# Sliding-window attention and a gated MLP on one core: f16 transposes for q and k, loads a stage earlier, and a new order at the end of batch 0

## The chip, the cores and the metric

The kernel runs on one NeuronCore of a Trainium2 chip. The metric is the device time of one execution in microseconds. Eleven executions of the kernel before are given, with their median; beside them one execution was taken with the hardware profiler.

## What is computed

Eight batches of 576 tokens and eight heads of 64. Attention looks back over 64 tokens; its output is the input of a gated MLP whose gate mixes tokens with a 576 x 576 matrix.

```python
scores = (1/sqrt(64)) * q @ k.T               # per batch and head, 576 x 576
mask = (rel >= 0) & (rel < 64)                # rel = query position - key position
attn = softmax(where(mask, scores, -1e9))
x = (attn @ v)                                # heads side by side: 576 x 512
h = relu(x @ w_in)                            # 576 x 1024
u, w = h[:, :512], h[:, 512:]
w_n = (w - mean(w)) / sqrt(var(w) + 1e-6)     # per token
out = (u * (w_spatial @ w_n + b_spatial)) @ w_out
```

## The kernel before

**Units of work.** All matmuls are f16 with fp32 sums. For each batch the program has these units, named by the letters of its order strings:

- T (`emit_T`, L287): q and k of two heads are brought to the layout with the 64 head elements on partitions. T0 to T3 take a pair of heads' first 512 tokens, T4 the last 64 tokens of all. In batches 0 to 3 (`NPE` is 4, L60) this is done on TensorE. `load_four` (L82) lets each partition hold four neighbouring tokens, so slot t of partition p is token 4p + t. `T_mm` (L258) multiplies each slot's 128 x 128 block with the identity and writes fp32 to PSUM with a step of four, which restores the order of tokens; k and q have a PSUM tile each. `T_out` (L277) copies k with VectorE and q with ScalarE into the f16 tile `tr`. In batches 4 to 7 the DMA brings another layout and VectorE turns 32 x 32 blocks (`turn`, L144; its units are T in stage 3 and R later).
- A (`att`, L582): scores S, exp on ScalarE and mask on VectorE of one head pair, and with it P (`emit_P`, L388), the product with v, of the pair before, then its normalisation: Ln (`emit_N1`, L411) and exp (`N_exp`) on ScalarE, a product on VectorE (`N_mul`, L426), which writes `x`. P has one PSUM buffer `oz`, S one buffer `sc`. What of the normalisation is left is done by the next unit, or by F.
- V (`emit_V`, L472; in parts as p for `V_mm`, L451, and o for `V_out`, L462): the half of w_in that is normalised, relu on ScalarE and `bn_stats` on VectorE. Q (`emit_VO4`, L481) is the last 64 tokens of V, run beside those of the batch before's O. L (`emit_LN`, L503): normalisation, five `vn` on VectorE.
- U (L520): the ungated half. W (`emit_W`, L571): transposes of w_spatial, once, in batch 0. G (L539): the product with w_spatial and the gate. O (L561): the product with w_out, a ScalarE copy to `ob` (five buffers), a store from SyncE.

All PSUM tiles of T, V, U, G, O and W come from one ring `mm` of four banks.

**Order.** Nothing is planned by a scheduler: every engine runs its instructions in program order (`manual_schedule`, L40), and waits only for semaphores. A first loop (L671) runs the attention of batch 0, with some idle matmuls `warm` in between. After it L706 to L721 interleave the rest of batch 0 with the attention of batch 1. Then stage a (L723) runs the MLP of batch a with the attention of batch a + 1, by a string of units for each a (`run`, L600).

**Loads.** q, k and v of a batch are loaded by DMAs from SyncE's queue (`load_pairs`, L96, for the first four; `load_batch`, L133, for the others: 16 DMAs of q and k, five of v). GpSimd casts them to f16 and makes a copy of v that is shifted by 64 partitions (`batch_in`, L654). The fp32 buffers and those of v are double; the f16 buffers of q and k (`nk`, `nq`) are single, so a cast waits until T of the batch before has read its own. Batches 0 and 1 are loaded at once, 2 before L704; for batch a + 2 the unit Q of stage a issues load and casts (L627). The weights come by GpSimd's DMAs (`load_win`, L238; `load_wsp`, L242). SyncE's queue also carries the stores.

Of the kernel before, what the change touches and what calls it, by code (L numbers as in the profile page):

```python
# [13 lines left out]
B = 8  # L14
# [5 lines left out]
def kernel(  # L20
# [11 lines left out]
    nc = tc.nc  # L32
    f16 = dt.float16
    f32 = dt.float32
# [12 lines left out]
    psp = ctx.enter_context(tc.tile_pool(name="ps", bufs=1, space=bass.MemoryType.PSUM))  # L47
# [59 lines left out]
    def pairs_in(b, s, copy_k, copy_q):  # L107
        cast_four(b, "k", s, copy_k)
        cast_four(b, "q", s, copy_q)
# [128 lines left out]
    def load_win(half):  # L238
        cs = slice(512 * half, 512 * half + 512)
        nc.gpsimd.dma_start(w_in_sb[:, :, cs], moe_w_in[:, cs].rearrange("(r p) c -> p r c", p=128))  # L240
# [15 lines left out]
    TP = {}  # L256

    def T_mm(b, s):  # L258
        if s < 4:
            tp = [psp.tile([128, 512], f32, tag="mm", bufs=4, name=f"tp{b}_{s}{x}") for x in "kq"]  # L260
        else:
            tp = psp.tile([128, 512], f16, tag="mm", bufs=4, name=f"tp{b}_{s}")
        TP[b, s] = tp
        with nc.named_scope(f"T{b}_{s}"):
            for y, x in enumerate("kq"):
                w = NH[b, x, s]
                if s < 4:
                    o = tp[y][:, :].rearrange("p (n t) -> p t n", t=4)
                    for t in range(4):
                        nc.tensor.matmul(o[:, t, :], w[:, 128 * t:128 * t + 128], id16[:, :],  # L270
                                         start=True, stop=True)
                else:
                    for p in range(4):
                        nc.tensor.transpose(tp[:, 256 * y + 64 * p:256 * y + 64 * p + 64],
                                            w[0:64, 128 * p:128 * p + 128], id16[0:64, 0:64])

    def T_out(b, s):  # L277
        tp = TP.pop((b, s))
        o = TR[b][:, :, :].rearrange("p x (a n) -> p x a n", a=4)
        for y in (0, 1):  # L280
            if s < 4:
                (act_copy if y == 1 else dve_copy)(o[:, y, s, 0:512], tp[y][:, :])
            else:
                nc.vector.tensor_copy(o[:, y, :, 512:576],
                                      tp[:, 256 * y:256 * y + 256].rearrange("p (a n) -> p a n", a=4))
# [102 lines left out]
    def emit_P(b, s):  # L388
        oz = psp.tile([128, 2, 512], f32, tag="oz", bufs=1, name=f"oz{b}_{s}")
        OZ[b, s] = oz  # L390
        e2 = E2.pop((b, s))
        Vn, Vs = V16[b]
        n = 512 if s < 4 else 256
        with nc.named_scope(f"P{b}_{s}"):
            for h in (0, 1):
                nc.tensor.matmul(oz[64 * h:64 * h + 64, 1, 0:n], onesK[:, :], e2[:, h, 0:n],  # L396
                                 start=True, stop=True)
            for u in range(8 if s < 4 else 4):
                c0 = 64 * u if s < 4 else slot(b, u)
                for h in (0, 1):  # L400
                    if s < 4:
                        hh = 2 * s + h
                        vt = Vn[:, u // 2, hh, :] if u % 2 == 1 or u == 0 else Vs[:, u // 2, hh, :]
                    else:
                        vt = Vs[:, 4, 2 * u + h, :]
                    nc.tensor.matmul(oz[64 * h:64 * h + 64, 0, c0:c0 + 64],  # L406
                                     vt, e2[:, h, c0:c0 + 64], start=True, stop=True)
# [163 lines left out]
    def emit_W(kk):  # L571
        sn = 128 if kk < 4 else 64
        wps = psp.tile([128, 1024], f16, tag="mm", bufs=4, name=f"wps{kk}")
        for tch in range(5):
            tn = 128 if tch < 4 else 64
            nc.tensor.transpose(wps[0:sn, 128 * tch:128 * tch + tn],
                                wsp_nat[0:tn, tch, 128 * kk:128 * kk + sn], id16[0:tn, 0:tn])
        (act_copy if kk % 2 else dve_copy)(wspT[kk][0:sn, 0:576], wps[0:sn, 0:576])

    state = {"P": None, "post": []}  # L580

# [18 lines left out]
    def run(a, seq):  # L600
        for t in seq.split():
            c, n = t[0], int(t[1:] or 0)
            if c == "A":
                if a + 1 < B:
                    att(a + 1, n)
            elif c == "T":
                if a + 1 < NPE:
                    emit_T(a + 1, n)
                elif a + 1 < B:
                    for x in "kq":  # L610
                        turn(a + 1, x, n)
            elif c == "R":
                if a + 2 < B:
                    for x in "kq":
                        turn(a + 2, x, n)
            elif c == "F":
                for f in state["post"]:
                    f()
                state["post"] = []
            elif c == "p":  # L620
                V_mm(a + n // 1000, n // 100 % 10, n // 10 % 10, n % 10)
            elif c == "o":
                V_out(a, n)
            else:
                if c == "Q":
                    emit_VO4(a)
                    if a > 0 and a + 2 < B:  # L627
                        load_any(a + 2)
                        batch_in(a + 2)
                elif c == "L":  # L630
                    emit_LN(a)
                elif c == "W":
                    emit_W(n)
                else:
                    UNIT[c](a, n)
                if state["post"]:
                    state["post"].pop(0)()

    def load_any(b):
        if b < NPE:  # L640
            load_pairs(b)
        else:
            new_qkv(b)
            load_batch(b)

    def v_in(b, s):
        if s < 4:
            cast_v_pair(b, s, pool_copy)
            shift_pair(b, s, pool_copy)
        else:  # L650
            cast_v_chunk(b, 4, pool_copy)
            shift_rem(b, pool_copy)

    def batch_in(b):  # L654
        if b < NPE:
            for s in range(4):
                pairs_in(b, s, pool_copy, pool_copy)
                if s == 3:
                    pairs_in(b, 4, pool_copy, pool_copy)
                v_in(b, s)  # L660
            v_in(b, 4)
            return
        for hp in (0, 1):
            for x in "kq":
                cast_qk(b, x, hp, pool_copy)
        for c in range(5):
            cast_v_chunk(b, c, pool_copy)
            if c in (1, 3, 4):
                shift_part(b, c // 2, pool_copy)

    for s in range(4):  # L671
        pairs_in(0, s, dve_copy, pool_copy if s < 3 else dve_copy)
        if s == 3:
            pairs_in(0, 4, pool_copy, pool_copy)
        v_in(0, s)
        if s == 2:
            load_win(1)
            load_win(0)
        T_mm(0, s)
        if s < 3:  # L680
            warm(2)
        if s > 0:
            E_mask(0, s - 1)
        if s > 1:
            N_mul(0, s - 2)
        T_out(0, s)
        emit_S(0, s)
        E_exp(0, s)
        if s == 3:
            T_mm(0, 4)  # L690
        if s > 0:
            emit_P(0, s - 1)
            emit_N1(0, s - 1)
            N_exp(0, s - 1)
        if s < 3:
            warm(4)
# [6 lines left out]
    load_pairs(2)  # L703
    batch_in(1)  # L704

    run(0, "p0002 p0102")  # L706
    emit_P(0, 3)
    emit_S(0, 4)
    E_exp(0, 4)
    emit_N1(0, 3)  # L710
    emit_N2(0, 3)
    E_mask(0, 4)
    run(0, "p0202 p0302")
    emit_P(0, 4)
    run(0, "p0023 p0123 p0223 p0323 p0034 o0 p0134 o1 p0234 o2 p0334 o3")
    emit_N1(0, 4)
    emit_N2(0, 4)
    run(0, "U0 U1 Q L U2 T0 U3 A0 W0 W1 W2 W3 W4 U4 G0 T1 A1 G1 G2 T2 G3 A2 G4")
    batch_in(2)
    run(0, "O0 O1 T3 A3 O2 O3 T4 F A4 F p1002 p1102")  # L720
    run(0, "A5 p1202 p1302 p1023 p1123 p1223 p1323 F")  # L721
# [1 line left out]
    for a in range(1, B):  # L723
        if a == 1:
            run(a, "p0034 o0 p0134 o1 p0234 o2 p0334 o3 T0 U0 T1 U1 A0 Q L T2 U2 U3 A1 U4 G0 T3 A2 "
                   "G1 G2 T4 A3 G3 A4 G4 O0 O1 A5 O2 O3")
        elif a == 2:
            run(a, "V0 T0 V1 T1 A0 V2 V3 Q T2 A1 F L U0 U1 U2 T3 A2 U3 U4 G0 T4 A3 G1 G2 G3 A4 "
                   "G4 O0 O1 A5 O2 O3")
        elif a == 3:  # L730
            run(a, "V0 T0 V1 V2 V3 A0 Q F L T1 U0 U1 A1 U2 U3 U4 A2 G0 G1 A3 G2 G3 A4 G4 R0 O0 O1 "
                   "A5 O2 R1 O3")
        else:
            run(a, "V0 V1 A0 V2 V3 Q A1 F L U0 U1 U2 A2 U3 U4 G0 A3 G1 G2 G3 A4 G4 R0 O0 O1 A5 O2 R1 O3")
# [31 lines left out]
```

The softmax here doesn't subtract the row's maximum and nothing guards it: scores larger than these inputs give would overflow.

## Time and profile before

| | |
|---|---|
| median of 11 runs | 242.35 us (240.89 to 246.01) |
| the profiled execution | 245.4 us |
| its span, first to last instruction | 243.7 us |
| granted TensorE clock, mean | 0.958 |
| busy: TensorE, VectorE, ScalarE, GpSimd | 215.1, 153.9, 157.8, 114.4 us |
| DMA: q1 (SyncE's queue), of 16 engines' span | 69.9% |
| stages 1 to 6, from one Q to the next | 25.45, 24.48, 24.72, 23.58, 28.95, 22.42 us |

PE is TensorE, PEld its weight loads, DVE VectorE, ACT ScalarE, POOL GpSimd, SP SyncE. [...] A wait is the idle time of an engine ahead of an instruction, with the instruction that released it. The chain of waits follows the last instruction back to what released each step.

### The profile page before, as it was taken

How to read it: one execution, taken by the hardware profiler on the slowest of the kernel's cores; microseconds unless marked ns; L12 is line 12 of the kernel's file. 1: busy time of each engine (PE TensorE's matmuls, PEld its weight loads, DVE VectorE, ACT ScalarE, POOL GpSimd, SP SyncE). 2: the span in 40 equal slices, each digit the busy share in tenths (PEclk: the TensorE clock that was granted, in tenths of full speed). 3: DMA queues.
4: the chain of work that ended last, by engine and by line, in shares of the span. 5: the costliest groups of instructions: out<-in, count | busy, mean ns of one | idle time of the engine just before them, and what ended most of it. 6: DMA issues, size and time to landing. Idle time of an engine off the chain costs nothing.

```text
span 243.7 us, 6712 instructions
## 1 busy us (share of the span) xinstructions
PE 215.1 (88%) x2727; PEld 116.6 (48%) x2727; DVE 153.9 (63%) x313; ACT 157.8 (65%) x283; POOL 114.4 (47%) x162
## 2 busy tenths in 40 slices
PE   7974874989789989999997999899959999999993
PEld 2642322655445645555545554455424645554451
DVE  6483158357347872878488679666955778774650
ACT  2573263447758957896777767957746578957713
POOL 3899339796420389304394349442863492000000
PEclk9997699599999999999999999999967999999999
DMA  6999999996300999169988997799889962004105
GB/s 181 300 189 187 238 253 185 263 258 108 135 0 3 258 252 230 41 146 200 194 245 166 192 190 236 153 192 177 258 179 193 186 185 65 3 4 173 24 0 194
DMA packets 77647, 40.43 MB, mean 166 GB/s; under 512 B 44272, under 2 KB 73008, under 8 KB 77616
## 3 DMA queue, kind: packets, MB, share of 16 engines
q1 hardware_dynamic: 75392, 37.76, 69.9%
q0 software_dynamic: 2224, 2.24, 5.6%
q8 instruction: 21, 0.34, 0.7%
q14 instruction: 10, 0.08, 0.2%
HBM read 32.79 MB, written 9.44 MB: 173 GB/s over the span
## 4 chain that ended last, share of the span: by engine, by line
PE 49%; DMA 16%; ACT 10%; POOL 8%; DVE 8%; SPq 4%; issue 4%; POOLq 0%; ACTq 0%
DMA fq<-in_q_dram 10%; PE ps L546 10%; PE po L565 8%; PE pv L459 8%; PE pu L526 6%; POOL vs L177 4%; DMA win<-in_moe_w_in_dram 3%; POOL vn L177 3%; PE oz L396 3%; SPq L117 3%; ACT e L361 2%; PE oz L406 2%; DMA vf<-in_v_dram 2%; DVE x L431 2%; DVE st L468 2%
## 5 line engine op out<-in xcount | busy, mean ns | idle before, releaser
L177 POOL COPY vs<-vn 64x512 f16<-64x512 f16 (+1 forms) x56 | 43.8, 783 | 3.1
L431 DVE TENSOR_TENSOR x<-oz,zi 128x512 f16<-128x512 f32 (+1 forms) x40 | 25.4, 635 | 30.4 <-ACT zi L423 30.1
L361 ACT ACTIVATE e<-sc 128x1024 f16<-128x1024 f32 x32 | 32.9, 1028 | 14.6 <-PE sc L303 10.6
L177 POOL CAST nk<-fk 128x512 f16<-128x512 f32 (+2 forms) x24 | 19.3, 804 | 48.3 <-DMA fk<-in_k_dram 35.1
L377 DVE TENSOR_TENSOR e<-e,mask 128x1024 f16<-128x1024 f16 x32 | 25.2, 788 | 21.9 <-ACT e L361 21.9
L546 PE MATMUL ps<-wspT,vn 128*128 128x512 f16 (+1 forms) x160 | 38.2, 385 | 0.0
L459 PE MATMUL pv<-win,x 128*128 128x512 f16 (+1 forms) x132 | 33.1, 395 | 4.8 <-DMA win<-in_moe_w_in_dram 3.0
L526 PE MATMUL pu<-x,win 128*128 128x512 f16 x128 | 33.2, 404 | 0.0
L468 DVE BATCH_NORM_STATS2 st<-vs 128x6 f32<-128x512 f16 (+1 forms) x40 | 26.9, 673 | 8.9 <-ACT vs L466 8.8
L177 POOL CAST nq<-fq 128x512 f16<-128x512 f32 (+2 forms) x27 | 21.3, 789 | 23.7 <-DMA fq<-in_q_dram 23.4
L177 POOL CAST vn<-vf 128x512 f16<-128x512 f32 (+1 forms) x40 | 26.0, 655 | 12.4 <-DMA vf<-in_v_dram 11.4
L466 ACT ACTIVATE vs<-pv 128x512 f16<-128x512 f32 (+1 forms) x40 | 23.2, 597 | 13.0 <-PE pv L459 11.0
L565 PE MATMUL po<-wout,g 128*128 128x512 f16 x128 | 30.1, 379 | 0.0
L549 DVE TENSOR_TENSOR g<-ps,ru 128x512 f16<-128x512 f32 x32 | 22.0, 687 | 7.5 <-PE ps L546 7.3
L568 ACT COPY ob<-po 128x512 f32<-128x512 f32 x32 | 18.7, 586 | 12.2 <-PE po L565 12.2
L414 ACT ACTIVATE ln<-oz 128x512 f32<-128x512 f32 (+1 forms) x40 | 22.4, 559 | 4.9 <-PE oz L406 4.8
L423 ACT ACTIVATE zi<-ln 128x512 f32<-128x512 f32 (+1 forms) x40 | 23.7, 591 | 0.9
L546 PEld LDWEIGHTS <-vn 128*128 128x128 f16 (+1 forms) x160 | 14.6, 99 | 15.8 <-issue 0.8
L459 PEld LDWEIGHTS <-x 128*128 128x128 f16 (+1 forms) x132 | 12.5, 101 | 19.4 <-DMA win<-in_moe_w_in_dram 3.1
L528 ACT ACTIVATE ru<-pu 128x512 f32<-128x512 f32 x32 | 17.9, 599 | 2.9 <-PE pu L526 2.5
L526 PEld LDWEIGHTS <-win 128*128 128x128 f16 x128 | 12.3, 104 | 14.8 <-issue 4.3
L516 DVE TENSOR_SCALAR vn<-vs,mv,rs 128x512 f16<-128x512 f16 (+1 forms) x40 | 16.4, 477 | 2.4 <-ACT rs L508 2.4
(93 smaller groups left out, 303.8 us busy)
## 6 DMA issues: line engine op xcount, KB each, us to landing
out_dram<-ob SPq DMA_DIRECT2D x32, 256.0 KB, 3.2
vf<-in_v_dram SPq DMA_DIRECT2D x40, 128.0 KB, 5.3
fk<-in_k_dram SPq DMA_DIRECT2D x32, 144.0 KB, 4.2
fq<-in_q_dram SPq DMA_DIRECT2D x32, 144.0 KB, 5.6
fk<-in_k_dram SPq DMA_DIRECT2D x16, 256.0 KB, 4.9
fq<-in_q_dram SPq DMA_DIRECT2D x16, 256.0 KB, 5.2
vf<-in_v_dram SPq DMA_DIRECT2D x16, 256.0 KB, 7.2
win<-in_moe_w_in_dram POOLq DMA_DIRECT2D x2, 512.0 KB, 9.3
```

Source lines behind the costliest of these rows:

```text
L177: nc.gpsimd.tensor_copy(o, i)
L361: nc.scalar.activation(e2[:, :, :], sc[0][:, :, :], AF.Exp, bias=0.0, scale=0.125)
L377: nc.vector.tensor_tensor(e2[:, :, :], e2[:, :, :], m, ALU.min)
L414: nc.scalar.activation(lnz[:, 0:n], OZ[b, s][:, 1, 0:n], AF.Ln)
L423: nc.scalar.activation(zinv[:, 0:n], lnz[:, 0:n], AF.Exp, bias=0.0, scale=-1.0)
L431: nc.vector.tensor_tensor(x[:, 0:n], oz[:, 0, 0:n], zinv[:, 0:n], ALU.mult)
L459: nc.tensor.matmul(PV[b, j][0:jn, :], xcol(b, r, j), w_in_sb[:, r, 512:1024], start=(r == 0), stop=(r == 3))
L466: nc.scalar.activation(vs[0:jn, :], pv[0:jn, :], AF.Relu)
L468: nc.vector.bn_stats(st6[0:jn, 0:6], vs[0:jn, :])
L526: nc.tensor.matmul(pu[:, :], w_in_sb[:, r, 128 * m:128 * m + 128], X[b, r][:, :], start=(r == 0), stop=(r == 3))
L546: nc.tensor.matmul(ps[:, :], VN[b, kk][0:kn, 128 * m:128 * m + 128], wspT[kk][0:kn, 0:512], start=(kk == 0), stop=(kk == 4))
L565: nc.tensor.matmul(po[:, :], G[b, r][:, 128 * j:128 * j + 128], w_out_sb[:, r, :], start=(r == 0), stop=(r == 3))
```

## The change

It has three parts.

1. `T_mm` takes f16 transposes, which write each slot's block unstepped into one f16 PSUM tile for k and q together; `T_out` reads that tile with a step of 128 elements and so restores the order of tokens.
2. From batch 4 on, load and casts are issued a stage earlier: those of batch 4 at the end of stage 1, those of a + 3 at Q of stage a from 2 on. Batch 3 stays where it was.
3. In batch 0, S and exp of the last 64 tokens go ahead of the first V matmuls, one half of w_in is asked for earlier, V's parts and the units U to W are put in another order, and `emit_W` copies three of its five parts with ScalarE in place of two. The strings of stages 1 and 3 change too.

```diff
     def T_mm(b, s):
-        if s < 4:
-            tp = [psp.tile([128, 512], f32, tag="mm", bufs=4, name=f"tp{b}_{s}{x}") for x in "kq"]
-        else:
-            tp = psp.tile([128, 512], f16, tag="mm", bufs=4, name=f"tp{b}_{s}")
+        tp = psp.tile([128, 1024], f16, tag="mm", bufs=4, name=f"tp{b}_{s}")
         TP[b, s] = tp
+        n = 512 if s < 4 else 256
...
-                if s < 4:
-                    o = tp[y][:, :].rearrange("p (n t) -> p t n", t=4)
-                    for t in range(4):
-                        nc.tensor.matmul(o[:, t, :], w[:, 128 * t:128 * t + 128], id16[:, :],
-                                         start=True, stop=True)
...
+                for t in range(4):
+                    if s < 4:
+                        nc.tensor.transpose(tp[:, n * y + 128 * t:n * y + 128 * t + 128],
+                                            w[:, 128 * t:128 * t + 128], id16[:, :])
...
-                (act_copy if y == 1 else dve_copy)(o[:, y, s, 0:512], tp[y][:, :])
+                (act_copy if y == 1 else dve_copy)(
+                    o[:, y, s, 0:512].rearrange("p (n t) -> p n t", t=4),
+                    tp[:, 512 * y:512 * y + 512].rearrange("p (t n) -> p n t", t=4))
...
-        (act_copy if kk % 2 else dve_copy)(wspT[kk][0:sn, 0:576], wps[0:sn, 0:576])
+        (act_copy if kk < 3 else dve_copy)(wspT[kk][0:sn, 0:576], wps[0:sn, 0:576])
...
                 if c == "Q":
                     emit_VO4(a)
-                    if a > 0 and a + 2 < B:
-                        load_any(a + 2)
-                        batch_in(a + 2)
+                    if a == 1:
+                        load_any(3)
+                        batch_in(3)
+                    elif 1 < a and a + 3 < B:
+                        load_any(a + 3)
+                        batch_in(a + 3)
...
+        if s == 2:
+            load_win(1)
         v_in(0, s)
         if s == 2:
-            load_win(1)
             load_win(0)
...
-    run(0, "p0002 p0102")
-    emit_P(0, 3)
     emit_S(0, 4)
     E_exp(0, 4)
+    run(0, "p0002 p0102 p0202 p0302")
+    emit_P(0, 3)
     emit_N1(0, 3)
     emit_N2(0, 3)
     E_mask(0, 4)
-    run(0, "p0202 p0302")
+    run(0, "p0023 p0123 p0223 p0323 p0034 o0 p0134 o1")
     emit_P(0, 4)
-    run(0, "p0023 p0123 p0223 p0323 p0034 o0 p0134 o1 p0234 o2 p0334 o3")
     emit_N1(0, 4)
     emit_N2(0, 4)
-    run(0, "U0 U1 Q L U2 T0 U3 A0 W0 W1 W2 W3 W4 U4 G0 T1 A1 G1 G2 T2 G3 A2 G4")
+    run(0, "p0234 o2 p0334 o3")
+    run(0, "U0 U1 T0 U2 Q A0 F U3 L W0 W1 W2 W3 W4 U4 T1 G0 A1 G1 G2 T2 G3 A2 G4")
...
         if a == 1:
             run(a, "p0034 o0 p0134 o1 p0234 o2 p0334 o3 T0 U0 T1 U1 A0 Q L T2 U2 U3 A1 U4 G0 T3 A2 "
-                   "G1 G2 T4 A3 G3 A4 G4 O0 O1 A5 O2 O3")
+                   "G1 G2 A3 T4 G3 G4 A4 O0 O1 A5 O2 O3")
+            load_any(4)
+            batch_in(4)
...
         elif a == 3:
-            run(a, "V0 T0 V1 V2 V3 A0 Q F L T1 U0 U1 A1 U2 U3 U4 A2 G0 G1 A3 G2 G3 A4 G4 R0 O0 O1 "
+            run(a, "T0 V0 V1 A0 V2 V3 Q A1 F L T1 U0 U1 U2 U3 A2 U4 G0 A3 G1 G2 G3 A4 G4 R0 O0 O1 "
                    "A5 O2 R1 O3")
```

More of the change, by code (lines that the diff above doesn't have):

```diff
@@ L266, in T_mm @@
                 w = NH[b, x, s]
-                if s < 4:
-                    o = tp[y][:, :].rearrange("p (n t) -> p t n", t=4)
-                    for t in range(4):
-                        nc.tensor.matmul(o[:, t, :], w[:, 128 * t:128 * t + 128], id16[:, :],
-                                         start=True, stop=True)
[L272 to L275, printed above, removed]
+                for t in range(4):
+                    if s < 4:
+                        nc.tensor.transpose(tp[:, n * y + 128 * t:n * y + 128 * t + 128],
+                                            w[:, 128 * t:128 * t + 128], id16[:, :])
+                    else:
+                        nc.tensor.transpose(tp[:, n * y + 64 * t:n * y + 64 * t + 64],
+                                            w[0:64, 128 * t:128 * t + 128], id16[0:64, 0:64])
     def T_out(b, s):
```

## The prediction

> **What bounds the kernel now.** I read the page first, then the stages, then PE's waits, then the chain, then the DMA queue of SyncE. A stage here runs from one start of the mixed group L493/L495 (`emit_VO4`) to the next; these starts are at 75.86, 101.31, 125.79, 150.51, 174.09, 203.04 and 225.46 us in PE's timeline. The stage view gives, in its columns, length, busy time of PE, PEld, DVE, ACT and POOL, granted clock, DMA share and GB/s:
> ```profile
> 0.00:19.98 19.98, 16.01 (x188) 9.30 (x188) 12.22 (x41) 9.80 (x13) 14.42 (x29) 1.00 0.99 219
> 19.98:47.52 27.54, 17.98 (x147) 9.21 (x146) 12.82 (x25) 11.58 (x23) 17.84 (x29) 0.78 1.17 227
> ...
> 174.09:203.04 28.95, 25.88 (x356) 13.03 (x355) 19.97 (x35) 18.75 (x34) 18.67 (x22) 0.88 0.91 196
> 203.04:225.46 22.42, 22.07 (x323) 11.73 (x322) 14.48 (x31) 17.21 (x33) 0.00 (x0) 1.00 0.16 55
> ```
> The stage of 22.42 us loads nothing and PE is full in it: that is what a late stage costs when only PE limits it. The one before takes 28.95 us for the same work. The end of batch 0 (19.98 to 47.52) holds 18 us of PE in 27.5, at a clock of 0.78. PE's waits name the places:
> ```profile
> PE sc L303 <- DVE tr L180: 5.6, 4, 3.5
> PE oz L406 <- POOL vs L177: 3.8, 3, 1.9
> PE oz L396 <- DVE x L431: 3.4, 5, 1.1
> PE pv L459 <- DMA win<-in_moe_w_in_dram: 3.0, 1, 3.0
> ```
> The longest (3.5) is S of batch 1 behind five `vn`; the 3.8 is P of later batches behind the V casts. The chain in order of time shows both, and the transposes:
> ```profile
> 14.91 8.07 DMA win<-in_moe_w_in_dram
> ...
> 38.43 3.43 DVE vn L516 x5
> 41.85 0.61 DVE tr L180
> 42.51 0.64 PE sc L303 x13
> 43.15 3.58 PE wps L576 x25
> ...
> 49.47 0.44 PE tp_1k L270 x4
> ...
> 57.89 1.73 PE po L565 x8
> ...
> 109.75 0.47 PE pu L532 x16
> ```
> [...] in windows of 5 us the granted clock is
> ```profile
> 175.00:180.00 5.00, 1.93 (x53) 1.32 (x52) 3.18 (x7) 2.32 (x4) 4.75 (x6) 0.87 0.71 217
> 180.00:185.00 5.00, 5.00 (x14) 1.52 (x13) 3.15 (x6) 2.70 (x6) 1.88 (x3) 0.50 1.18 197
> ```
> 0.66 and 0.65 at 20 to 30 us and 0.71 and 0.61 at 40 to 50 as well: each time about 6.8 us at half speed ((0.34+0.35) x 5 / 0.5 = 6.9).
>
> [...] the L270 matmuls write fp32 with a step of four and take 0.44/4 = 110 ns for 128 columns, while 512 contiguous columns take 1.73/8 = 216 and 64 take 0.47/16 = 29, so 128 should take 29 + 187 x 64/448 = 56. [...]
>
> **The change, part by part.** The sum is made against the profiled execution, 245.4 us (span 243.7 and 1.7 around it), which lies 3.05 above the median of 242.35.
>
> *Transposes (T).* Eight matmuls of 110 ns become eight f16 transposes. Bounds: 56 ns (contiguous) and 110 (no gain); I take 56, since the 64-column f16 transposes L274 already run at 0.12/4 = 30 ns. That is 0.43 us per T. The copies: DVE (676 ns) and ACT (589) now read f16 with a step of 128 elements. No row shows a stepped PSUM read. [...] I take the present durations[...]. [...] I expect that q's copy (ACT) waits for k's (DVE), and k's for all eight transposes. Behind the waiting ACT copy stand E_exp and N1; who waits for it is S. Bounds: 0 and 0.6 us per T; I take 0.6 where T and S stand close. In batch 0's loop S recurs each 4.02 us (10.61, 14.63, 18.65), a ring of S, exp 1.02, mask, N_mul 0.69, k copy 0.68; q's copy was hidden in it and now joins: 0.27 + 0.57 + 0.6 + 0.6 = **+2.0**. In the rest of batch 0's stage T2 and T3 have one group or none before their S: the 0.43 is eaten by the copies, 0. Of T0, T1 before the first mixed group, four T in stage 1 and two in stage 2, PE is full around them: 8 x 0.43 = **-3.4**. T also takes one of the four `mm` buffers in place of two; no wait of size is on them, so 0.
>
> *Batch 0's end.* `load_win(1)` goes ahead of POOL's cast and two shifts of v: issued at about 12.6 in place of 14.91, so with the same 8.07 landed at 20.7. It holds POOL 0.87 us, and v of pair 2 is needed only at 15.2: nothing. By program order (S4 first, at 20.2, after exp of s=3): eight V matmuls (1.73) 20.7 to 22.4; P3 22.4 to 23.0 (its buffer frees when DVE's x, 21.32 + 0.69, is done); ln, exp, N_mul 0.6+0.65+0.7: x3 at 25.1 (28.78 before); P4 at 25.6; x4 at 28.1, since two bn_stats of 0.8 now stand behind it (35.16 before). U0, U1, T0, U2 and Q's group follow to 30.4. T0's copies go ahead of LN, S of batch 1 at 31.1 (42.51 before): the 3.5 us wait goes. vs4 at 32.1, its statistics 33.0, LN's scalars 34.1, five `vn` 3.43 to 37.5. W's 25 transposes fit between 32.3 (the spatial weights land at 21.39 + 10.2 = 31.6) and 35, hidden under `vn`; three copies on ACT (0.64) run meanwhile, two on DVE behind `vn` to 38.5. So the first G group ends at 38.7, not 49.3: **-10.6**, with the clock full. What is late next is `vn`: PE idles about 2 us before G0 and is thin from 32 on, so I expect one half-clock period again; G's first group costs 1.1 more, and what is full until it ends some 1.6: **+2.7**. Batch 1's casts (last shift done at 48.2) and batch 2's (bound by T3 and T4 of batch 1) keep their distance, as their users were at 54 and later.
>
> *Order in stage 1.* T4 between A3 and G3, G4, and A4 after G4 put 1.8 us of G ahead of P, which waited 1.13 on N_mul at 90.45: **-0.9**.
>
> *Loads.* Sixteen q, k and five v DMAs on SP and nine casts and shifts on POOL move. Load 4 goes from behind the store of the next stage (104.24) to behind O3's (about 96.4): 8 us; loads 5, 6, 7 move a stage. They pass on SP the stores of a whole stage, on POOL nothing but each other. POOL's casts of batch 5 wait for the turns of batch 4 (one `nk`, `nq` buffer); only batch 6's casts are queued behind, needed 20 us later. From the first mixed group at 0 the stages then begin at 0, 23, 46, 69, 92, 115, and loads of 18 to 19 us with 4 us of stores end at about 41, 60, 82, 103 for batches 4 to 7; P of these needs them, with 5 us of V work on POOL, at 47, 70, 92, 115. PE's POOL waits of 0.7 and 3.1 (the 3.8 above), the DVE `tr` waits of 0.36 and 1.15 and the half clock after them go. Three stages of 24.72, 23.58 and 28.95 become 22.9 each (23.58 less its 0.68 wait): **-8.5**, and -0.4 in stage 2. Against it stand SP's stores: five `ob` buffers, each stage's stores issued only when the next load is through, landing about 60, 83 and 105 while the same buffers are wanted at 62, 85 and 107. I allow 0 to 2 us, taken as **+1**. T0 ahead of V0 in stage 3 costs nothing: PE has V0 beside it.
>
> Sum: 245.4 + 2.0 - 3.4 - 10.6 + 2.7 - 0.9 - 8.5 - 0.4 + 1 = **227.3**; I say 227.
>
> **The rivals.** *Short copies, full clock*: q's copy does not wait, or the G0 gap is too short to halve the clock: 227.3 - 2.0 - 2.7 = 222.6. For it: by the working above PE is busy two thirds of the time up to 31 us. *Slow stepped reads*: [...] 233. [...] *DMA sets the stage*: load and stores take 25 us a stage in place of 22.9, and one half clock (3.3) stays: 227.3 + 6.3 - 1 + 3.3 = 236. For it: a DMA share near 1.2 during loads. *Transposes are no faster*: 230.7. *Slower, by stores behind loads*: if the `ob` buffers come back late, ACT's copy of O0 stops, `mm` buffers stay full and PE stops; after an idle stretch (1.2 us at 18.65 did not halve the clock, 3.1 at 178 did: I take 2 us) half a clock period follows, 2 + 3.3 us in each of four stages: 227.3 + 21 = 248. It decides from 2 us more than my 2 us of slack. The change plainly does what it says, apart from the speed of T.
>
> **The numbers.** Forecast (224 to 230) 0.48; short copies 0.15; slow reads 0.15; DMA 0.13; transposes 0.05; stores 0.04. The range from 221 to 236 leaves out the slow case and the edges. Half a per cent, 1.2 us, is about what a measurement of this kernel tells from no change; only the edge of the DMA case (0.02) lies there.
>
> **What would show it.** Right: L270's group 0.22 us for four; S of batch 0 each 4.6 us; first G group near 39 to 43; three stages near 23; no P wait on `vs`; stores landing late. Wrong: ACT `tr` starting beside DVE's (then 2 us less), copies over 1 us, `ob` L568 or the stores' waits growing with PE idle at O0.

## The result, and the profile after

The changed kernel takes 247.28 us (median of 12 executions, 244.79 to 251.89) against 242.90 for the kernel before (47 executions). The ratio is 1.0188, 95% interval [1.0155, 1.0221]: slower by 1.9%, where 227 was forecast. The profiled execution took 247.61 us with a span of 245.9. Ratios, here and below, leave out the slow executions of a kernel, and the profiled executions of the kernel before (245.4 us) and of two experiments (`e4_before_loads`, `e5_before_end`) were such slow ones, so that a stretch of theirs shows where time goes, while what a part is worth is taken from the ratios.

The stages, with the same columns as before (length, busy time of PE, PEld, DVE, ACT, POOL, granted clock, DMA share, GB/s). The first line is the end of batch 0 up to the first G group, which took from 19.98 to 47.52 before; then come stages 1 to 5:

```profile
22.30:40.97 18.67, 15.54 (x155) 8.32 (x154) 11.46 (x24) 12.06 (x25) 12.78 (x21) 0.91 1.20 231
68.54:100.15 31.61, 25.13 (x313) 14.08 (x307) 16.73 (x32) 18.55 (x35) 15.13 (x24) 0.89 0.72 176
100.15:130.09 29.94, 25.24 (x315) 13.72 (x314) 19.87 (x38) 20.72 (x37) 13.01 (x14) 0.94 1.15 194
130.09:156.78 26.69, 24.26 (x356) 13.18 (x356) 19.30 (x38) 18.39 (x34) 15.79 (x17) 0.94 1.09 230
156.78:181.01 24.23, 23.19 (x355) 12.34 (x355) 20.32 (x36) 18.09 (x34) 13.53 (x15) 1.00 0.99 207
181.01:205.24 24.23, 23.18 (x355) 12.33 (x354) 20.33 (x36) 18.09 (x34) 10.75 (x12) 1.00 0.16 56
```

Of the kernel before, stages 1 and 2:

```profile
75.86:101.31 25.45, 24.07 (x315) 14.15 (x307) 16.71 (x34) 19.72 (x35) 15.31 (x24) 1.00 0.71 187
101.31:125.79 24.48, 24.12 (x315) 13.35 (x315) 17.48 (x36) 18.66 (x34) 8.13 (x9) 1.00 0.89 178
```

The end of batch 0 is 9 us shorter, and the first mixed group (Q of stage 1, with which that stage begins) stands at 68.54 in place of 75.86: so far the forecast's sum came true. Stages 1 and 2, 25.45 and 24.48 before, are 31.61 and 29.94. (In `e5_before_end`, whose program is that of the kernel before in these stages, they take 25.44 and 24.48.) Stage 5 lost 4.7 us; stages 3 and 4 did not become 22.9.

The waits (engine, its line, what it waited for: total us, times, longest us) name the place:

```profile
ACT tr L183 <- DVE tr L180: 28.6, 15, 5.2
...
PE sc L301 <- ACT tr L183: 11.9, 10, 2.2
...
PE sc L317 <- DVE tr L147: 2.6, 2, 2.4
...
PE ps L544 <- ACT tr L183: 2.3, 1, 2.3
```

The first line did not exist before: ScalarE stands for 28.6 us in front of q's copy (L183) until VectorE has made k's (L180). The longest of these waits, 5.25 us, is ScalarE's idle start, ahead of the first copy; the other 14 come to 23.3 us. The POOL waits of P on `vs` (3.8 us before) are gone. What one of the 14 does is seen in the timeline of the changed kernel (start, length, engine, line, operation; in brackets the idle time ahead and its releaser):

```profile
72.67 1.70 DVE L514 TENSOR_SCALAR vn<-vs,mv,rs 128x512 f16<-128x512 f16 x5 [0.61 <-ACT rs L506]
...
74.29 0.68 DVE L180 COPY tr<-tp 128x512 f16<-128x512 f16 x1
...
75.01 0.59 ACT L183 COPY tr<-tp 128x512 f16<-128x512 f16 x1 [2.37 <-DVE tr L180]
...
75.49 1.09 ACT L526 ACTIVATE ru<-pu 128x512 f32<-128x512 f32 x2
75.64 1.24 PE L544 MATMUL ps<-wspT,vn 128*128 128x512 f16 x5 [2.27 <-ACT tr L183]
```

k's copy is queued on VectorE behind five `vn`. ScalarE has reached q's copy and idles 2.37 us, with two relus of finished U groups queued behind it. PE has filled the four `mm` buffers with T2, U2, U3 and U4; G0 wants the buffer of T2, whose last reader is q's copy, and PE idles 2.27 us. A half clock follows: the granted clock, the third figure from the end, is 0.65 and 0.63 in these windows (0.50 from 77 to 83 us):

```profile
75.64:80.00 4.36, 3.00 (x33) 1.94 (x34) 1.89 (x3) 3.13 (x6) 2.31 (x5) 0.65 1.00 267
80.00:85.00 5.00, 5.00 (x50) 2.22 (x48) 3.42 (x6) 2.79 (x5) 4.76 (x9) 0.63 1.06 267
```

The chain of waits of after, against the one shown of before: the weight load of 8.07 us and the 3.58 us of W's transposes have left it; `vn` stays, and k's and q's copies in series and the turn of batch 4 are new.

```profile
37.55 3.01 DVE vn L514 x5
...
74.37 0.61 DVE tr L180
75.01 0.59 ACT tr L183
...
136.91 1.36 DVE tr L147 x2
138.31 1.06 PE sc L317 x28
```

### The profile page after: what moved, and what is told of

Its sections match the earlier page's. It is cut to its first block, busy times and chain, and to the rows that moved or that the text cites. A ratio compares the mean times of both kernels' runs of the same rounds, so it can differ in the third digit from the quotient of the medians.

```text
span 245.9 us, 6707 instructions
## 1 busy us (share of the span) xinstructions
PE 209.0 (85%) x2727; PEld 112.6 (46%) x2727; DVE 158.2 (64%) x312; ACT 156.4 (64%) x284; POOL 116.5 (47%) x162
## 4 chain that ended last, share of the span: by engine, by line
PE 44%; DVE 19%; ACT 19%; DMA 7%; SPq 5%; issue 4%; ACTq 0%
PE ps L544 9%; PE po L563 9%; PE pv L457 9%; ACT e L359 6%; DVE vn L514 5%; DMA fk<-in_k_dram 4%; DVE x L429 4%; ACT zi L421 3%; PE oz L394 3%; SPq L130 3%; ACT tr L183 3%; DVE tr L180 3%; SPq L117 2%; DVE st L466 2%; DMA vf<-in_v_dram 2%
## 5 line engine op out<-in xcount | busy, mean ns | idle before, releaser
L177 POOL COPY vs<-vn 64x512 f16<-64x512 f16 (+1 forms) x56 | 44.6, 797 | 3.1
L375 DVE TENSOR_TENSOR e<-e,mask 128x1024 f16<-128x1024 f16 x32 | 26.9, 842 | 29.0 <-ACT e L359 29.0
L544 PE MATMUL ps<-wspT,vn 128*128 128x512 f16 (+1 forms) x160 | 41.0, 401 | 5.1 <-ACT tr L183 2.3
L177 POOL CAST nk<-fk 128x512 f16<-128x512 f32 (+2 forms) x24 | 20.4, 850 | 51.9 <-DVE tr L147 26.2
L177 POOL CAST vn<-vf 128x512 f16<-128x512 f32 (+1 forms) x40 | 26.7, 678 | 10.2 <-DMA vf<-in_v_dram 9.4
L524 PE MATMUL pu<-x,win 128*128 128x512 f16 x128 | 30.3, 380 | 0.0
L183 ACT COPY tr<-tp 128x512 f16<-128x512 f16 x16 | 9.4, 586 | 28.6 <-DVE tr L180 28.6
L566 ACT COPY ob<-po 128x512 f32<-128x512 f32 x32 | 18.7, 585 | 12.0 <-PE po L563 11.7
L412 ACT ACTIVATE ln<-oz 128x512 f32<-128x512 f32 (+1 forms) x40 | 22.3, 559 | 6.1 <-PE oz L404 6.1
L544 PEld LDWEIGHTS <-vn 128*128 128x128 f16 (+1 forms) x160 | 15.2, 102 | 23.9 <-issue 7.6
L514 DVE TENSOR_SCALAR vn<-vs,mv,rs 128x512 f16<-128x512 f16 (+1 forms) x40 | 19.5, 553 | 1.4 <-ACT rs L506 1.4
L394 PE MATMUL oz<-e,onesK 128*64 128x512 f16 x64 | 13.7, 420 | 6.6 <-DVE x L429 6.4
```

The costliest lines, as they stand in the source:

```text
L177: nc.gpsimd.tensor_copy(o, i)
L375: nc.vector.tensor_tensor(e2[:, :, :], e2[:, :, :], m, ALU.min)
L514: nc.vector.tensor_scalar(vn[0:jn, :], vs[0:jn, :], mv[0:jn, j, 0:1], rs[0:jn, j:j + 1], ALU.subtract, ALU.mult)
L524: nc.tensor.matmul(pu[:, :], w_in_sb[:, r, 128 * m:128 * m + 128], X[b, r][:, :], start=(r == 0), stop=(r == 3))
L544: nc.tensor.matmul(ps[:, :], VN[b, kk][0:kn, 128 * m:128 * m + 128], wspT[kk][0:kn, 0:512], start=(kk == 0), stop=(kk == 4))
```

## The experiments

The theory after seeing this: the loss is the shared PSUM tile, which puts ScalarE's copy behind VectorE's (the 28.6 us above). Rivals: the stepped reads or the transposes themselves; the loads and casts a stage ahead; the new order. Ratios are to the kernel before, measured beside it.

| run | what it is | median us | ratio, 95% interval |
|---|---|---|---|
| e1_split | after, two tiles | 231.88 | 0.9501 [0.9414, 0.9587] |
| e2_before_tshared | before + transposes, shared tile | 255.41 | 1.0474 [1.0387, 1.0562] |
| e3_before_tsplit | before + transposes, two tiles | 244.17 | 0.9971 [0.9907, 1.0035] |
| e4_before_loads | before + loads and strings | 243.47 | 1.0025 [0.9992, 1.0058] |
| e5_before_end | before + end of batch 0 | 232.95 | 0.9539 [0.9422, 0.9656] |
| e6_after_told | after, old transposes | 233.54 | 0.9538 [0.9444, 0.9632] |
| e7_shared_dve | after, both copies on VectorE | 235.04 | 0.9667 [0.9586, 0.9748] |
| e8_split_t1 | e1, turn ahead of `vn` | 231.78 | 0.9521 [0.9466, 0.9575] |
| e9_split_gate | e1, casts held behind `vn` | 228.73 | 0.9391 [0.9334, 0.9449] |
| e10_split_t1_gate | e1 with both | 226.06 | 0.9307 [0.9255, 0.9358] |
| e11_told_t1_gate | e10, old transposes | 227.03 | 0.9370 [0.9319, 0.9420] |
| e12_split_oldloads | e1, loads and strings of before | 227.92 | 0.9383 [0.9329, 0.9437] |

**Is it the shared tile?**

```diff
-        tp = psp.tile([128, 1024], f16, tag="mm", bufs=4, name=f"tp{b}_{s}")
+        if s < 4:
+            tp = [psp.tile([128, 512], f16, tag="mm", bufs=4, name=f"tp{b}_{s}{x}") for x in "kq"]
...
-                    tp[:, 512 * y:512 * y + 512].rearrange("p (t n) -> p n t", t=4))
+                    tp[y][:, :].rearrange("p (t n) -> p n t", t=4))
```

> The changed kernel with k's and q's transposes in two PSUM tiles again (two `mm` buffers per T, f16), all else as changed. Theory (the loss is q's copy on ACT waiting for k's on DVE, because both halves lie in one tile): ACT's waits on `tr <- DVE tr` fall from 28.6 us to under 5, stages 1 and 2 fall from 31.6 and 29.9 to about 24 each, batch 0's loop goes back to about 4.0 us a pair, and the time to about 232 (67 to the first mixed group, stages 24, 24, 26.7, 24.2, 24.2, 22.4, and 18.2 + 1.7). Rivals (the stepped reads, the loads moved ahead or the new order are at fault): stages 1 and 2 stay near 30, time 244 to 248.

Measured 231.88. Stages 1 and 2 are 25.84 and 24.36, S of batch 0 recurs each 4.02 us, the first mixed group stands at 64.05. ScalarE no longer waits for VectorE's copy at all, and PE's waits for S are small (first the two stages, then waits):

```profile
64.05:89.89 25.84, 22.55 (x315) 12.91 (x307) 16.78 (x35) 19.61 (x35) 15.39 (x24) 1.00 0.81 210
89.89:114.25 24.36, 23.59 (x315) 12.81 (x314) 18.53 (x38) 19.03 (x34) 13.44 (x14) 1.00 1.14 197
...
ACT tr L183 <- PE tp_0q L269: 5.3, 1, 5.3
...
PE sc L303 <- DVE tr L180: 4.3, 5, 1.6
...
PE sc L303 <- ACT tr L183: 1.0, 2, 0.7
```

(The 5.3 are ScalarE's idle start.) So one tile in place of two turns a gain of 5% into a loss of 2%. The same part alone, on the kernel before, with its rival and with the old transposes in the changed kernel (the edits: `T_mm` and `T_out` of the change; of the diff above; of the kernel before):

```diff
e2, on before: T_mm and T_out as in the change
e3, on before: T_mm and T_out as in e1
e6, on after:  T_mm and T_out as in before
```

> The kernel before with the change's transposes and copies alone (one shared tile; order and loads as before). Theory (serial copies): ACT waits over 20 us on `tr <- DVE tr`, stages 1 and 2 grow by 4 to 6 us each and the loop of batch 0 by 0.6 a pair: about 253. Rivals (loads or order at fault, the transposes a gain): 243 less 3.4 = about 240.

> The kernel before with f16 transposes and stepped copies in two separate tiles; order and loads as before. Theory: the transposes save 8 x 0.43 us where PE is full and nothing waits on the copies, about 240. Rival (stepped PSUM reads hurt[...]): 243 or more.

> The changed kernel with the old fp32 matmul transposes and contiguous copies (order and loads as changed). Theory: the order and the loads are a gain on their own: about 235 (the split version's 232 and 3.4 of slower transposes), stages 1 and 2 near 25. Rivals (loads or order at fault): stages 1 and 2 stay near 30, time about 247.

Measured 255.41, 244.17 and 233.54. With the shared tile the kernel before loses 12.0 us (255.41 - 243.44); with two tiles there is neither gain nor loss clear of the noise. That is less than the 3 us of the theory, and within what the rival of slow reads expected (243 or more); but reading with a step is not slow (678 ns on VectorE and 586 on ScalarE in the changed kernel, 676 and 589 before), and stages 1 and 2 of e3 take 25.11 and 24.42, no longer than before. So e3 leaves the gain of the transposes open, and speaks only against a loss. Without the new transposes the change is a gain: order and loads are not what made it slower.

**Is it S coming later, or ScalarE's queue standing still?** With both copies on VectorE, one behind the other in the shared tile, S still has to wait for both of them, but no waiting copy stands in ScalarE's queue:

```diff
-                (act_copy if y == 1 else dve_copy)(
+                dve_copy(
```

> The changed kernel, one shared tile as in it, but q's copy on DVE too, right behind k's: S of each pair can start no sooner than in the changed kernel, and DVE does 16 copies of 0.67 us more, but ACT has nothing to wait for. Theory (the loss is ACT's queue of relu and exp standing behind the waiting copy): stages 1 and 2 fall to about 26, time about 236 to 238. Rival (the loss is S itself coming a copy later, whoever makes it): 246 to 250.

Measured 235.04. S waits for the copies as long as in the changed kernel, 11.7 us in 10 waits against 11.9 in 10. ScalarE's idle time did not go either: it now lies ahead of exp, for S (28.1 us, of which 6.7 are its idle start), where no relu that PE needs is held up by it:

```profile
ACT e L359 <- PE sc L301: 28.1, 13, 6.7
...
PE sc L301 <- DVE tr L180: 11.7, 10, 2.2
```

The first mixed group stands at 68.47, where the changed kernel has it (68.54): up to there ScalarE's copy costs no more than a second copy on VectorE, and both lose 4.4 to 6.0 us to two tiles. (The program of e1 up to there is also that of e9 and e10, which like these two had one period of half clock there; the group stands at 64.05, 62.43 and 63.08 in them.) But the next two stages are whole again:

```profile
68.47:94.70 26.23, 22.57 (x313) 13.11 (x306) 19.40 (x39) 17.74 (x30) 15.63 (x24) 1.00 0.83 213
94.70:118.92 24.22, 23.50 (x316) 12.80 (x316) 19.90 (x40) 18.14 (x32) 13.27 (x14) 1.00 1.09 195
```

31.61 + 29.94 - 26.23 - 24.22 = 11.1 us came back, although VectorE does 16 copies of 0.675 us more (its group of `tr<-tp` has x32 in place of x16). The 11.1 us were ScalarE's queue standing behind q's copy, with the half clocks that followed: by the granted clocks of 0.89 and 0.94, about 5 of the 11.1 (31.61 x 0.11 + 29.94 x 0.06).

**What are the other parts worth alone?**

```diff
e4, on before: load and casts as in the change, and its strings of stages 1 and 3
-                    if a > 0 and a + 2 < B:
-                        load_any(a + 2)
-                        batch_in(a + 2)
+                    if a == 1:
+                        load_any(3)
+                        batch_in(3)
+                    elif 1 < a and a + 3 < B:
+                        load_any(a + 3)
+                        batch_in(a + 3)
e5, on before: the lines of batch 0's loop and string, and of emit_W, as in the change
...
-        (act_copy if kk % 2 else dve_copy)(wspT[kk][0:sn, 0:576], wps[0:sn, 0:576])
+        (act_copy if kk < 3 else dve_copy)(wspT[kk][0:sn, 0:576], wps[0:sn, 0:576])
```

> The kernel before with the loads, casts and strings of stages 1 to 3 of the change alone (old transposes, old end of batch 0). The forecast counted 9.8 us for these (8.5 + 0.4 + 0.9): 233. Theory from the traces so far: stage 5 falls from 28.9 to 24.2, but stages 3 to 5 stay at 24 to 26, since the turn of batch 4 stands behind `vn` and POOL's casts now lie beside `vn`: 3 us in all, about 240.

> The kernel before with the end of batch 0 of the change alone (string, place of the weight load, engine of the W copies; old transposes and loads). Forecast and theory: the first G group near 38.7 in place of 47.5 and the first mixed group 11 us earlier, all later stages as before: about 232. Rival (what is won there is lost to later stalls, as loads and casts then come too late for stages 1 and 2): 238 or more.

Measured 243.47 and 232.95. The end of batch 0 is nearly the whole gain, 10.3 us (243.29 - 232.95) of the 11.6 by which e1 is ahead (243.44 - 231.88). Loads and strings alone are worth nothing that the medians show: in e4, PE's waits on `vs` are gone and stage 5 is 24.2, but stage 3 holds a wait of 2.42 us at 134.67, S behind the turn (L147), with half a clock after it (0.83 granted in this stage); and stages 4 and 5 each hold a wait of 0.70 for `vn`. The changed kernel has the same waits (138.31, 166.26, 190.49).

**Why are stages 3 to 5 not 22.9?** In e1's stages 4 and 5, with POOL casting next to it, VectorE's five `vn` take 4.33 us (their durations summed; neighbours overlap a little, so that a timeline shows 4.01); in stage 6, with POOL idle, 2.01. The timeline of VectorE in e1's stage 4:

```profile
144.40 1.53 DVE L377 TENSOR_TENSOR e<-e,mask 128x1024 f16<-128x1024 f16 x1 [0.76 <-ACT e L361]
145.85 0.68 DVE L431 TENSOR_TENSOR x<-oz,zi 128x512 f16<-128x512 f32 x1
146.45 4.01 DVE L516 TENSOR_SCALAR vn<-vs,mv,rs 128x512 f16<-128x512 f16 x5
150.39 0.67 DVE L377 TENSOR_TENSOR e<-e,mask 128x1024 f16<-128x1024 f16 x1
```

The mask product of 1.53 us lies beside a POOL shift from 144.35 to 145.39; the same product takes 0.67 at 150.39. Three edits on e1 test this: the turn ahead of `vn` (T1 before L), the casts held back until `vn` is done, and both.

```diff
e8:
-            run(a, "T0 V0 V1 A0 V2 V3 Q A1 F L T1 U0 U1 U2 U3 A2 U4 G0 A3 G1 G2 G3 A4 G4 R0 O0 O1 "
+            run(a, "T0 V0 V1 A0 V2 V3 Q A1 F T1 L U0 U1 U2 U3 A2 U4 G0 A3 G1 G2 G3 A4 G4 R0 O0 O1 "
e9:
...
                         load_any(a + 3)
-                        batch_in(a + 3)
                 elif c == "L":
                     emit_LN(a)
+                    if 2 < a and a + 2 < B:
+                        pool_copy(gate[:, :], VN[a, 4][0:1, 0:1])
+                        batch_in(a + 2)
```

> The version with two tiles (231.9 us), and in stage 3 the second turn of batch 4 ahead of the five `vn` (T1 before L). Theory: PE's wait of 2.43 us on `tr L147` and the half clock after it (1.7) go: stage 3 from 26.8 to about 23.5, time about 229. Rival (`vn` 1.5 us later holds up G instead): 231 to 232.

> The version with two tiles (231.9 us), with POOL's casts of batches 5, 6 and 7 held back by one tiny copy of `vn` until `vn` of stages 3, 4 and 5 is done. Theory [...]: `vn` is 0.40 us each in stages 4 and 5 in place of 0.53 to 1.18, and each of these stages falls from 24.25 to about 22.9: about 229. Rival (the casts' place costs nothing, or they hit the mask products just as hard): 231 to 232.

> Both together (T1 before L, and the casts behind `vn`), on the version with two tiles. Theory: the two gains add: stages 3, 4, 5 near 23.3, 22.9, 22.9, about 226. Rival (they overlap, or neither is real): 229 or more.

Measured 231.78, 228.73 and 226.06. The gate alone does nearly what was expected: `vn` is 0.40 us each again, and stages 4 and 5 fall from 24.25 to 23.29 each, though not to 22.9. So of the 2.3 us by which `vn` was longer a stage paid 1.0. (The intervals of e1 and e9 overlap a little.) The line of `vn` in stage 4 of e9 (shortest, median and longest in ns):

```profile
L517 DVE TENSOR_SCALAR vn<-vs,mv,rs x5: 402/407/409, 144.4 to 145.6; 128x512 f16<-128x512 f16 x4, 64x512 f16<-64x512 f16 x1
```

The earlier turn alone gains nothing, and the reason given for the rival was not the right one. The turn sets POOL's casts free, which now fall on `vn` in stage 3 as well (e8):

```profile
L516 DVE TENSOR_SCALAR vn<-vs,mv,rs x5: 691/1226/1229, 118.1 to 122.3; 128x512 f16<-128x512 f16 x4, 64x512 f16<-64x512 f16 x1
```

PE then waits for `vn` at 121.25 and 122.40 in place of for the turn. With the gate, that way is shut and the turn gains another 2.7 us (228.73 - 226.06; the intervals just overlap, but stage 3 goes from 26.75 to 24.27). The gate on top of the turn, e10 against e8, is 5.7 us and clear of the noise. e10 beats both kernels; its stages 3 to 5 are the nearest to the forecast's 22.9:

```profile
113.25:137.52 24.27, 22.85 (x355) 12.21 (x354) 20.32 (x38) 18.32 (x34) 13.40 (x15) 1.00 1.10 225
137.52:160.81 23.29, 22.85 (x355) 12.34 (x354) 19.14 (x36) 18.21 (x34) 13.24 (x15) 1.00 1.10 220
160.81:184.10 23.29, 22.85 (x355) 12.31 (x354) 19.15 (x36) 18.21 (x34) 13.24 (x15) 1.00 0.43 131
```

**What are transposes and loads worth once nothing else stands in the way?**

```diff
e11, on e10: T_mm and T_out as in before
e12, on e1:  load and casts, and the strings of stages 1 and 3, as in before
```

> The version of 226.1 us (two tiles, T1 before L, casts behind `vn`) with the old fp32 transposes and contiguous copies. Theory (the f16 transposes save 0.43 us per T where PE is full): stages 1 and 2 longer by 1.7 and 0.9, the stretch to the first mixed group by 1: about 229. Rival (the gaps beside the transposes swallow what they save, as in the comparison of the kernel before with its two-tile form, ratio 0.997): 226 to 227.

> The version with two tiles (231.9 us) with loads, casts and strings of stages 1 to 3 as in the kernel before; new are the transposes and the end of batch 0 alone. Theory (moving the loads pays nothing as long as the casts lie beside `vn`): 231 to 233, stage 5 near 27 to 29, stages 3 and 4 near 26 and 23. Rival (the loads are worth what the forecast gave them): 239 or more.

Measured 227.03 and 227.92. e11 against e10 is 1.0 us, at the edge of what the rival expected; the intervals overlap. Stages 1 and 2 are longer by only 0.4 and 0.1. The first mixed group comes 1.0 us later (64.08 against 63.08), but that shows nothing: in e1, e8, e9, e10 and e12, whose programs are the same up to there, it stands anywhere from 60.71 to 64.05. e12 is a miss: its time is below what was expected in either case, since stage 5 took 24.52, not 27 to 29:

```profile
158.79:183.31 24.52, 23.08 (x355) 12.24 (x355) 18.36 (x35) 18.52 (x34) 13.78 (x16) 1.00 1.02 206
```

It has the same waits of P on `vs`, but of 0.59 and 0.85 us in stage 5 where the kernel before has 1.88 and 1.19, and no half clock follows. (In e2, also with the old loads, stage 5 took 24.03; in e5 it took 28.78.) So moving the loads, by itself, gains nothing on this version and if anything costs (227.92 without against e1's 231.88 with; the intervals overlap a little); with the gate and the earlier turn the two are 226.06 and 227.92, intervals overlapping.

## Why the prediction was wrong, step by step

The four stretches of its sum, in us, of the profiled executions (forecast from its own terms; the tail is unchanged):

| stretch | forecast | measured | off by |
|---|---|---|---|
| to the first mixed group: 2.0 - 0.86 - 10.6 + 2.7 | -6.8 | -7.3 | -0.6 |
| stage 1: -0.9 - 4 x 0.43 | -2.6 | +6.2 | +8.8 |
| stage 2: -0.4 - 2 x 0.43 | -1.3 | +5.5 | +6.7 |
| stages 3 to 5: -8.5 + 1 | -7.5 | -2.1 | +5.4 |

**The step that failed** is the price of the serial copy: "Bounds: 0 and 0.6 us per T; I take 0.6 where T and S stand close", and with it "PE is full around them", by which the T up to stage 2 got no price for the copies at all. The wait itself was foreseen, and its engine, and even the queue: "Behind the waiting ACT copy stand E_exp and N1". But the upper bound was the length of the copy waited for. The wait ends when VectorE has made k's copy, and ahead of that stand `bn_stats`, `vn`, `x` or the gate `g`: without ScalarE's idle start 23.3 us in 14 waits, 1.7 each and up to 2.5. And behind it on ScalarE stand also the relus that free PE's `mm` buffers, so that PE waits, not only S; for the one `mm` buffer of T, "no wait of size is on them, so 0" missed the 2.27 us of G0. e7 gives both sizes: late copies, whoever makes them, cost 4.4 to 6.0 us up to the first mixed group, the standing queue 11.1 in stages 1 and 2, of the 15.5 by which these are off. The other 4.4 are for the most part the gain of 3.9 (2.6 + 1.3) that the forecast put into these stages and that e10 doesn't show either: 25.80 and 24.37, against 25.45 and 24.48 before.

**Transposes, -3.4.** The duration was right: four start within 0.22 us (5.96, 6.19, 6.41). So was the reading with a step: 678 ns on VectorE and 586 on ScalarE, against 676 and 589. The gain was oversized: three pairs of runs give 0.7 us (before and e3, 0.3%), 1.7 (e1 and e6) and 1.0 (e10 and e11), none clear of the noise. In e10 PE waits 1.07 us for `x` at 70.90 where e11 waits 0.24 at 71.89; that such waits swallow the rest is likely but not shown.

**Batch 0's loop, +2.0**, was right: S recurs each 4.63 us (4.6 forecast). **Batch 0's end, -10.6**, was right in mechanism and about right in size: the first G group began at 40.97 and ended at 42.2 (38.7 forecast), in part since each T here also paid the serial copy, where the forecast had "0" (in e1 it begins at 38.81); alone, in e5, this part gains 10.3 us. **The half clock, +2.7**, did not come where it was forecast: around G0 (40.97) the granted clock was 1.00 from 35 to 45 us, though PE idled 1.20 us ahead of it. One period of 3.4 us, at 0.50 and so worth 1.7, came earlier, from 22.3 to 25.7 us beside the first V matmuls. So it is partly luck that this stretch is off by only 0.6 us.

**Order in stage 1, -0.9**: wrong in sign. The wait of 1.13 became two, 0.71 and 1.06 (e4: 90.62, 94.17), and the stage went from 25.45 to 26.17. Other runs agree: with the old transposes it takes 25.44 in the old order (e5), 26.38 and 26.21 in the new one (e6, e11).

**Loads, -8.5**: the waits that it removes went, the forecast of 22.9 did not come. "What is late next" was not asked there: the turn T1 behind `vn` (2.43 us and a half clock, 0.94 granted in stage 3), and POOL's casts beside `vn` (2.3 us a stage, of which the stage pays 1.0). Both could have been read in the profile before, where `vn` beside POOL's work in stage 5 has one of 1.26 us among its usual 0.40. Much of the 4.7 us won in stage 5 was a half clock (0.88 granted in it before), which e2 and e12 do not have even with the old loads.

**Stores, +1**: no wait of size; ScalarE's `ob` waits for PE alone (11.7 us). Of the rivals none was the cause; that the slower one ends near the measured time (248) is luck, as its mechanism did not occur. The test "ACT `tr` starting beside DVE's" pointed at the right place: q's copy starts 0.04 us after k's has ended (74.97, 75.01), so that the dependency was read rightly.

On the two tiles: with one tile for k and q, q's copy waits 15 times for k's, 28.6 us in all; in e1, with a tile for each, never. On the casts beside `vn`, in stage 4 of the changed kernel: a `vn` started at 163.93 beside a POOL shift of 1.03 us takes 1.18 (0.40 in stage 6, with POOL idle), while `bn_stats` stays at 0.66 beside the casts at 157.55, and `g` at 0.67 beside a shift at 167.33. The runs show these durations, and not what makes them.

## What to carry to other kernels

When two engines read one PSUM tile in turn, as k's and q's copies did here, the price was not the length of the first read (0.68 us): it was how late that engine got to it (a wait of 1.7 us on average, up to 2.5), for everything queued behind the second reader on its engine, here above all the relus that free PE's `mm` buffers. Give each reader its own tile (231.88 us here, in place of 247.28), or give both reads to one engine (235.04). Before moving GpSimd copies, look what VectorE will be doing at their new time (a `vn` took 0.40 us without them and up to 1.18 beside them in stage 4 of e1), and whether the wait that goes was also what kept them apart.

## What was not expected of the hardware

- Five `vn` of 128x512 f16 take 2.0 us with POOL idle and 4.3 with POOL copying; holding back POOL's casts by one wait took the time from 231.88 to 228.73 (e9) and, with the earlier turn, from 231.78 to 226.06 (e10).
- The two-tile kernel and its variants ran with hardly any half clock (e6, e11, e12: mean granted clock 0.998 each) or with one or two periods of 3.4 us (e1, e8, e9, e10: 0.983 to 0.992), for waits of PE that hardly differ: the 2.43 us wait on the turn is followed by half a clock of 3.4 us in e1 and in the changed kernel (0.94 granted in stage 3), and by none in e7 (1.00). So these runs don't tell from the length of a wait whether a half clock follows it. What sets one off is left open; a period of 3.4 us at 0.50 is worth 1.7 us.
- Reading f16 from PSUM with a step of 128 elements costs the same as reading fp32 in order (678 against 676 ns on VectorE, 586 against 589 on ScalarE).
